# Linear attention and a grouped mixture of experts: the token inputs of each expert take another way into their transposed layout

## The chip, the cores and the metric

One core of one Trainium2 chip. The time is device microseconds of one execution of the whole kernel.

## The reference

```python
def _attn_ref(q, k, v, g_norm):                    # 8 batches, 8 heads, 576 tokens, head size 64
    kv = np.einsum('bhsd,bhse->bhde', k, v)
    out = np.einsum('bhsd,bhde->bhse', q, kv)
    rms = np.sqrt(np.mean(out * out, axis=-1, keepdims=True) + 1e-06)
    return out / rms * g_norm

def _moe_ref(x, w_group, w_expert, w1, w2):        # x: 4608 tokens x 512
    # the group g of a token is the argmax of x @ w_group, its expert e the argmax of x @ w_expert[g];
    # g_w and e_w are the two softmax values of the chosen ones
    for g, e:                                      # 4 x 4 experts
        h = np.maximum(x[tokens] @ w1[g, e], 0.0)  # 512 -> 1024
        out[tokens] = (g_w * e_w)[:, None] * (h @ w2[g, e])   # 1024 -> 512
```

All inputs and the result are float32.

## The kernel before

The first part computes the attention, writes its unnormalised rows with their factors to a DRAM table `scr` (4609 rows of 520 floats), routes the tokens and orders the experts by their number of tokens. The second part, in which the change lies, takes the experts in that order as **regions** 0 to 15. Region r has a fixed capacity CAPS[r] (384, 364, 354, 330, 326, 312, 302, 300, 292, 290, 284, 274, 268, 264, 260, 256 tokens), so all sizes are known when the program is built; what is beyond the capacities goes through a loop at the end. Most of region 0 is done earlier, in plain float32; its last 128 tokens stand at the start of the second part.

Precision: weights and inputs are split into a high part (`whi`, `xh`, `hh`; cast on ScalarE) and a low part (`wlo`, `xl`, `hl`; a subtraction on VectorE), and each product is three matmuls (L305, L306, L310). TensorE does, in each region, layer 1 (8 output chunks f, 4 x 3 matmuls each) into `ps` and layer 2 (4 output chunks d, 8 x 3 matmuls each) into three `psy` buffers.

The order on every engine is the order in the source (a manual schedule); an instruction that waits holds all that stand behind it on its engine. In region r:

- **Inputs of region r + 1.** `gather(r)` fetches token rows from `scr` by three indirect DMAs on GpSimd into `xg` (two buffers). `scale` multiplies them by their factors on GpSimd (L276). `move_x` (L1249), 16 DMAs on SyncE of 32 partitions each, carries quarters of the features to quarters of the partitions, SBUF to SBUF, into `xq` (one buffer), so that `turn_x` (L1254, 32 x 32 block transposes on VectorE) makes the transposed inputs `xt` out of them. `split_x` makes `xh` (L1260) and `xl` (L1261).
- **Results of region r - 1.** `yq` (L1297, one buffer) is the block transpose of `psy` on VectorE; `move_y` (L1268), 16 DMAs on SyncE, brings the quarters back to token rows `yo`, and `scatter_rows` (L252, indirect DMAs on GpSimd) writes them to the result.
- **Weights.** `load_half` (L208) on SyncE loads a half of w1 or w2, 1 MB; `split_piece` (L241 on ScalarE, L242 on VectorE) splits a quarter of a matrix. All raw and split halves rotate through 12 buffers, so a load waits for the split of the half that it replaces.

In layer 2, chunk d is: `split_piece` of the next w1, then (d < 2) two `turn_x`, the matmuls, the `yq` transpose, then `split_x`. SyncE's order in a region is 16 `move_y`, 16 `move_x`, two loads of w2 (f = 3 and 5), two loads of w1 (d = 2 and 3). In region 0 the 16 moves for region 1 are issued in turn by SyncE and ScalarE.

Of the kernel before, what the change touches and what calls it, by code (L numbers as in the profile page):

```python
# [9 lines left out]
F32 = mybir.dt.float32  # L10
# [45 lines left out]
def tile_linattn_moe(ctx: ExitStack, tc: tile.TileContext, qm, qt, k, v, router, w1, w2, out):  # L56
# [27 lines left out]
    RW = DM + H  # L84
    scr = tc.dram_tile([NTOK + 1, RW], F32, name="scr")
    ovt = tc.dram_tile([NBLK, 4], F32, name="ovt")

# [1050 lines left out]
    with ExitStack() as ph:  # L1138
# [81 lines left out]
        def next_psy():  # L1220
            psys.append(psys.pop(0))
            return psys[-1]
# [4 lines left out]
        def moves(cap):  # L1227

            part = [slice(32 * i, 32 * i + 32) for i in range(4)]
            return [(a, s_, part[a], part[s_], len(range(s_, (cap + 31) // 32, 4)))  # L1230
                    for k in range(4) for s_ in range(4) for a in [(s_ + k) % 4]]
# [9 lines left out]
        def scale(r, g):  # L1241
            for j, _ in blocks(CAPS[r]):
                scale_rows(nc.gpsimd, g[0][:, j])

        def move_x(r, g, queues=(nc.sync,)):
            xq = mp.tile([P, 12, P], F32, name="xq", bufs=1)
            pq = xq.rearrange("p (j s) f -> p j s f", s=4)
            for i, (a, s_, pa, ps_, n) in enumerate(moves(CAPS[r])):
                queues[i % len(queues)].dma_start(pq[pa, 0:n, s_, :], g[0][ps_, 0:n, a * P:(a + 1) * P])  # L1249
            return xq, mp.tile([P, KC, 384], F32, name="xt", bufs=1)  # L1250
# [64 lines left out]
        for j, _ in blocks(CAPS[1]):  # L1315
            scale_rows(nc.vector, cur[0][:, j])
        nxt = gather(2)
        ps = next_psy()
        o, h1 = ps[:, 0:DM // 2], st["h"]["h"][:, :, P:2 * P]
# [4 lines left out]
        nc.scalar.activation(out=xT, in_=tp.rearrange("p (c t) -> p c t", c=KC), func=AF.Copy, scale=g2[:, 0:1])  # L1324
        xq, xt = move_x(1, cur, [nc.sync, nc.scalar])
        for i in range(2, 4):
            load_next(i)
        whole2(o, h1, w2c[1], lo=CUT)
# [10 lines left out]

        split_piece(w1n, 0)  # L1340
        for hf in range(2):
            ps = ps_h.tile([P, 512], F32, name="ps")
            whole1(ps, xT, w1c[hf])
            nc.scalar.activation(out=hr[:, hf * 512:(hf + 1) * 512], in_=ps, func=AF.Relu)
            for c in (2 * hf, 2 * hf + 1):
                turn_x(1, xq, xt, c)
                split_x(1, cur, xt, c)
        turn(0)
        turn(1)
        split_piece(w1n, 1)  # L1350
        for x in psys:
# [7 lines left out]
        scatter_rows(yo, P, gidx[:, 0, 2:3])  # L1359
        w1c, w2c = w1n, w2n  # L1360
        nw1, nw2, load_next = weight_loads(eidx[0:1, 2:3])
        for i in range(2):
# [5 lines left out]
        for r in range(1, NE):  # L1368
            cap = CAPS[r]
            _, xh, xl = cur  # L1370
            hh = mp.tile([P, FC, 384], F32R, name="hh", bufs=1)
            hl = mp.tile([P, FC, 384], F32R, name="hl", tag="hl", bufs=1)
            if todo:
                results = move_y(*todo)
            for f in range(FC):
# [7 lines left out]
                if r > 1:  # L1383
                    next(tables, None)
                    next(tables, None)
                if nxt and f == 0:
                    scale(r + 1, nxt)
                    xq, xt = move_x(r + 1, nxt)
                if nxt and f in (3, 5):
                    load_next((f + 1) // 2)  # L1390
                if f >= 3 and results:
                    scatter_rows(*results.pop(0))
                if f == FC - 1 and r + 1 == NE:
                    nc.gpsimd.drain()  # L1394
            nxt2 = gather(r + 2) if r + 2 < NE else None
            nw1a, nw2a, load_a = weight_loads(eidx[0:1, r + 2:r + 3]) if nxt2 else (None, None, None)
# [141 lines left out]
```

## Time and profile before

| | |
|---|---|
| Runs | median 697.4 us (693.17, 697.40, 699.06) |
| Profiled execution | 697.57 us, of which the span of the trace is 695.6 us |
| PE (TensorE matmul) busy | 582.1 us, 84% of the span |
| VectorE (DVE) busy | 368.9 us, 53% |
| ScalarE (ACT) busy | 266.8 us, 38% |
| GpSimd (POOL) busy | 191.4 us, 28% |
| Mean granted TensorE clock | 0.908 |

Busy time is time in which an engine executes; issuing a DMA is not counted. Times in timelines are microseconds from the start of the span. In a timeline line the square brackets tell how long the engine was idle before it and what ended the idleness. SPq and ACTq are the issue of DMAs by SyncE and ScalarE. The granted clock is the TensorE clock as a share of full speed. A DMA share is the mean busy share of the 16 DMA engines.

### The profile page before, as it was taken

How to read it: one execution, taken by the hardware profiler on the slowest of the kernel's cores; microseconds unless marked ns; L12 is line 12 of the kernel's file. 1: busy time of each engine (PE TensorE's matmuls, PEld its weight loads, DVE VectorE, ACT ScalarE, POOL GpSimd, SP SyncE). 2: the span in 40 equal slices, each digit the busy share in tenths (PEclk: the TensorE clock that was granted, in tenths of full speed). 3: DMA queues.
4: the chain of work that ended last, by engine and by line, in shares of the span. 5: the costliest groups of instructions: out<-in, count | busy, mean ns of one | idle time of the engine just before them, and what ended most of it. 6: DMA issues, size and time to landing. Idle time of an engine off the chain costs nothing. (4 is left out here: it accounts for less than half of the span.)

```text
span 695.6 us, 13526 instructions
## 1 busy us (share of the span) xinstructions
PE 582.1 (84%) x5199; PEld 537.0 (77%) x5199; DVE 368.9 (53%) x786; ACT 266.8 (38%) x534; POOL 191.4 (28%) x281
## 2 busy tenths in 40 slices
PE   8889789993799999696979796959696959687795
PEld 4677666871599999696979796959596959687795
DVE  3228868711277764654545545545456464637380
ACT  0356546211253443343434343333334343425260
POOL 4033232340080323223132323131313232221102
PEclk9888999997699999898989898989898989897988
DMA  9999994587036484838484838383838383837331
GB/s 307 379 384 394 335 348 131 198 254 285 0 104 251 117 301 107 301 96 273 116 297 116 310 90 302 96 284 111 291 108 303 91 303 95 300 101 280 89 135 66
DMA packets 74197, 146.95 MB, mean 211 GB/s; under 512 B 12370, under 2 KB 51618, under 8 KB 63122
## 3 DMA queue, kind: packets, MB, share of 16 engines
q1 hardware_dynamic: 65264, 123.51, 51.8%
q0 software_dynamic: 7824, 22.11, 11.2%
q8 instruction: 42, 0.69, 0.4%
q10 hardware_dynamic: 1042, 0.44, 0.3%
q14 instruction: 25, 0.20, 0.1%
HBM read 107.98 MB, written 19.54 MB: 183 GB/s over the span
## 5 line engine op out<-in xcount | busy, mean ns | idle before, releaser
L305 PE MATMUL psy<-hh,whi 128*128 128x364 f32 (+13 forms) x448 | 148.6, 332 | 73.2 <-DVE yq L1297 73.2
L242 DVE TENSOR_TENSOR wlo<-wr,whi 128x1024 fp32r<-128x1024 f32 (+1 forms) x180 | 151.5, 869 | 39.4 <-ACT whi L241 36.0
L305 PEld LDWEIGHTS psy<-hh,whi 128*128 128x128 f32 x448 | 95.1, 212 | 76.1 <-DVE yq L1297 76.0
L306 PE MATMUL psy<-hl,whi 128*128 128x364 f32 (+13 forms) x448 | 146.1, 326 | 0.0
L310 PE MATMUL psy<-hh,wlo 128*128 128x364 f32 (+13 forms) x448 | 145.1, 324 | 0.0
L306 PE MATMUL ps<-xl,whi 128*128 128x364 f32 (+14 forms) x480 | 144.6, 301 | 0.5 <-DVE xl L1261 0.5
L252 POOL DMA_INDIRECT out_dram<-yo,gall x45 | 49.2, 1094 | 346.7 <-DMA xq<-xg 282.7
L305 PE MATMUL ps<-xh,whi 128*128 128x364 f32 (+14 forms) x480 | 144.6, 301 | 0.0
L310 PE MATMUL ps<-xh,wlo 128*128 128x364 f32 (+14 forms) x480 | 144.0, 300 | 0.0
L241 ACT CAST whi<-wr 128x1024 fp32r<-128x1024 f32 (+1 forms) x180 | 128.6, 756 | 0.0
L1260 ACT ACTIVATE xh<-xt,rw 128x364 fp32r<-128x364 f32 (+14 forms) x60 | 32.6, 543 | 199.8 <-DVE xt L1254 199.8
L1254 DVE STREAM_TRANSPOSE xt<-xq 128x320 f32<-128x320 f32 (+4 forms) x60 | 27.1, 487 | 152.4 <-DMA xq<-xg 152.4
L306 PEld LDWEIGHTS psy<-hl,whi 128*128 128x128 f32 x448 | 95.5, 213 | 0.0
L310 PEld LDWEIGHTS psy<-hh,wlo 128*128 128x128 f32 x448 | 94.9, 212 | 0.0
L306 PEld LDWEIGHTS ps<-xl,whi 128*128 128x128 f32 x480 | 90.9, 189 | 0.9 <-DVE xl L1261 0.8
L305 PEld LDWEIGHTS ps<-xh,whi 128*128 128x128 f32 x480 | 90.9, 189 | 0.0
L310 PEld LDWEIGHTS ps<-xh,wlo 128*128 128x128 f32 x480 | 90.7, 189 | 0.0
L279 ACT ACTIVATE hh<-ps 128x364 fp32r<-128x364 f32 (+14 forms) x120 | 50.5, 421 | 101.1 <-PE ps L310 97.8
L280 DVE SCALAR_TENSOR_TENSOR hl<-ps,hh 128x364 fp32r<-128x364 f32 (+14 forms) x120 | 55.2, 464 | 46.8 <-ACT hh L279 46.1
L276 POOL TENSOR_TENSOR xg<-xg 128x256 f32<-128x256 f32 x82 | 52.7, 666 | 26.2 <-DMA xg<-scr,gall 24.5
L248 POOL DMA_INDIRECT xg<-scr,gall x44 | 44.4, 1009 | 13.3 <-issue 13.3
L367 PE MATMUL warm<-wide_b,ones_b 128*128 128x512 bf16 x142 | 42.2, 432 | 2.2 <-POOL wide_b L101 2.2
(255 smaller groups left out, 592.2 us busy)
## 6 DMA issues: line engine op xcount, KB each, us to landing
wr<-in_w_dram SPq DMA_DIRECT2D x64, 1024.0 KB
scr<-xo SPq DMA_DIRECT2D x36, 256.0 KB
m_q<-in_qm_dram SPq DMA_DIRECT2D x8, 1024.0 KB
m_k<-in_k_dram SPq DMA_DIRECT2D x7, 1024.0 KB
m_v<-in_v_dram SPq DMA_DIRECT2D x7, 1024.0 KB
yo<-yq SPq DMA_DIRECT2D x116, 48.0 KB
xq<-xg SPq DMA_DIRECT2D x108, 48.0 KB
xq<-xg SPq DMA_DIRECT2D x124, 32.0 KB
```

The source lines that it names most:

```text
L241: nc.scalar.copy(out=hi, in_=x)
L242: nc.vector.tensor_tensor(out=lo, in0=x, in1=hi.bitcast(F32), op=ALU.subtract)
L248: return nc.gpsimd.indirect_dma_start(out=xg[0:rows, 0:RW], out_offset=None, in_=src, in_offset=bass.IndirectOffsetOnAxis(ap=idx[0:rows, : ...
L252: sc = nc.gpsimd.indirect_dma_start(out=out, out_offset=bass.IndirectOffsetOnAxis(ap=idx[0:rows, :], axis=0), in_=yo[0:rows, :], in_offset ...
L276: eng.tensor_tensor(out=out_[:, hs], in0=x[:, hs], in1=factors(xg)[:, h], op=ALU.mult)
L279: nc.scalar.activation(out=hh, in_=ps, func=AF.Relu)
L280: nc.vector.scalar_tensor_tensor(out=hl, in0=ps, scalar=0.0, in1=hh.bitcast(F32), op0=ALU.max, op1=ALU.subtract)
L305: nc.tensor.matmul(ps, lhsT=stat_h(c), rhs=mov_h(c), start=(c == 0), stop=False)
L306: nc.tensor.matmul(ps, lhsT=stat_h(c), rhs=mov_l(c), start=False, stop=False)
L310: nc.tensor.matmul(ps, lhsT=stat_l(d), rhs=mov_h(d), start=False, stop=(d == n - 1))
L367: nc.tensor.matmul(st["warm"], lhsT=ones_b, rhs=wide_b, start=True, stop=True)
L1260: nc.scalar.activation(out=xh, in_=x, func=AF.Copy, scale=g2[:, 0:1])
```

## The change

A pair of DRAM tables `xd` takes the place of the SBUF-to-SBUF moves of the inputs. `put_x` writes the scaled rows of a region to one of them, 2 KB a row, in up to three DMAs; `get_x` reads `xq` from it in four, one for each quarter of the partitions, in pieces of 512 bytes. In the loop, `get_x(r + 1)` stands at the start of region r ahead of `move_y`; `gather(r + 2)` moves from the end of layer 1 to f = 0, and `scale(r + 2)` and `put_x(r + 2)` stand at f = 1, a region earlier than `scale` and `move_x` did. The scatters of the results begin at f = 5 in place of 3. In region 0, `put_x(1)`, `get_x(1)` and the loads of w2 stand ahead of `gather(2)`, `scale(2)` follows it, `turn_x` and `split_x` for region 1 follow both `turn` calls, `split_piece` of piece 1 moves into the loop over hf, and ScalarE issues none of the transfers. `move_y` stays as it is.

```diff
+    xd = [tc.dram_tile([3 * P, DM], F32, name=f"xd{i}") for i in range(2)]
...
-        def move_x(r, g, queues=(nc.sync,)):
+        def put_x(r, g):
+            for j, rows in blocks(CAPS[r] + -CAPS[r] % 32):
+                nc.sync.dma_start(xd[r % 2][j * P:j * P + rows, :], g[0][0:rows, j, 0:DM])
+
+        def get_x(r):
+            n = (CAPS[r] + 31) // 32
             xq = mp.tile([P, 12, P], F32, name="xq", bufs=1)
-            pq = xq.rearrange("p (j s) f -> p j s f", s=4)
-            for i, (a, s_, pa, ps_, n) in enumerate(moves(CAPS[r])):
-                queues[i % len(queues)].dma_start(pq[pa, 0:n, s_, :], g[0][ps_, 0:n, a * P:(a + 1) * P])
+            for a in range(4):
+                nc.sync.dma_start(xq[32 * a:32 * a + 32, 0:n, :],
+                                  xd[r % 2][0:32 * n, a * P:(a + 1) * P].rearrange("(b i) f -> i b f", i=32))
             return xq, mp.tile([P, KC, 384], F32, name="xt", bufs=1)
...
             scale_rows(nc.vector, cur[0][:, j])
+        put_x(1, cur)
+        xq, xt = get_x(1)
+        for i in range(2, 4):
+            load_next(i)
         nxt = gather(2)
+        scale(2, nxt)
...
-        xq, xt = move_x(1, cur, [nc.sync, nc.scalar])
-        for i in range(2, 4):
-            load_next(i)
...
-        split_piece(w1n, 0)
         for hf in range(2):
+            split_piece(w1n, hf)
             ps = ps_h.tile([P, 512], F32, name="ps")
             whole1(ps, xT, w1c[hf])
             nc.scalar.activation(out=hr[:, hf * 512:(hf + 1) * 512], in_=ps, func=AF.Relu)
-            for c in (2 * hf, 2 * hf + 1):
-                turn_x(1, xq, xt, c)
-                split_x(1, cur, xt, c)
         turn(0)
         turn(1)
-        split_piece(w1n, 1)
+        for c in range(KC):
+            turn_x(1, xq, xt, c)
+            split_x(1, cur, xt, c)
...
         w1c, w2c = w1n, w2n
+        put_x(2, nxt)
         nw1, nw2, load_next = weight_loads(eidx[0:1, 2:3])
...
+            if nxt:
+                xq, xt = get_x(r + 1)
             if todo:
                 results = move_y(*todo)
...
-                if nxt and f == 0:
-                    scale(r + 1, nxt)
-                    xq, xt = move_x(r + 1, nxt)
+                if f == 0:
+                    nxt2 = gather(r + 2) if r + 2 < NE else None
+                if nxt2 and f == 1:
+                    scale(r + 2, nxt2)
+                    put_x(r + 2, nxt2)
                 if nxt and f in (3, 5):
                     load_next((f + 1) // 2)
-                if f >= 3 and results:
+                if f >= 5 and results:
                     scatter_rows(*results.pop(0))
...
-            nxt2 = gather(r + 2) if r + 2 < NE else None
```

## Rows read from the trace of the kernel before

**Rows 1.** The page: busy time of TensorE (time, share of the span, instructions), and the granted TensorE clock in 40 equal slices of the span, in tenths.

```profile
PE 582.1 (84%) x5199; PEld 537.0 (77%) x5199; DVE 368.9 (53%) x786; ACT 266.8 (38%) x534; POOL 191.4 (28%) x281
...
PEclk9888999997699999898989898989898989897988
```

**Rows 2.** The list of waits over the whole span: who waited, for whom, us in total, times, the longest.

```profile
DVE xt L1254 <- DMA xq<-xg: 152.4, 14, 13.4
...
PE psy L305 <- DVE yq L1297: 73.2, 12, 8.2
```

**Rows 3.** The timeline of SyncE's issues in region 8 and into region 9: start, duration, line, transfer, number of issues.

```profile
433.91 10.25 SPq L1268 DMA_DIRECT2D yo<-yq  x16
444.34 11.24 SPq L1249 DMA_DIRECT2D xq<-xg  x16
456.56 8.41 SPq L208 DMA_DIRECT2D wr<-in_w_dram  x4
469.62 0.61 SPq L1268 DMA_DIRECT2D yo<-yq  x1
```

**Rows 4.** The timeline of VectorE in layer 2 of region 8: the first `xt`, the `yq` of the first chunk, the last `wlo` and the last `yq`.

```profile
460.73 0.91 DVE L1254 STREAM_TRANSPOSE xt<-xq 128x320 f32<-128x320 f32 x2 [13.20 <-DMA xq<-xg]
461.56 0.47 DVE L1297 STREAM_TRANSPOSE yq<-psy 128x320 f32<-128x320 f32 x1
...
467.94 1.22 DVE L242 TENSOR_TENSOR wlo<-wr,whi 128x1024 fp32r<-128x1024 f32 x1
469.08 0.51 DVE L1297 STREAM_TRANSPOSE yq<-psy 128x320 f32<-128x320 f32 x1
```

**Rows 5.** Windows: length, busy time (and instructions) of PE, PEld, DVE, ACT and POOL, granted clock, DMA share, GB/s. In this order: regions 1 to 3; after the stall of region 7; region 8; layer 1 of region 4.

```profile
185.40:284.00 98.60, 94.95 (x573) 93.78 (x572) 58.90 (x115) 38.79 (x69) 35.23 (x38) 1.00 0.55 167
...
426.40:431.00 4.60, 4.60 (x18) 4.60 (x19) 4.25 (x8) 3.33 (x6) 0.00 (x0) 0.50 0.95 362
431.93:466.83 34.90, 27.30 (x194) 27.06 (x193) 17.32 (x31) 12.34 (x24) 9.50 (x12) 0.90 0.62 191
...
292.25:306.64 14.39, 14.39 (x97) 14.39 (x97) 10.70 (x26) 6.55 (x14) 0.00 (x0) 1.00 0.43 129
```

**Rows 6.** The timeline of PE: the first matmul after the first, the fifth and the last of the twelve stalls in layer 2.

```profile
286.28 0.64 PE L305 MATMUL psy<-hh,whi 128*128 128x330 f32 x1 [5.42 <-DVE yq L1297]
...
426.38 0.62 PE L305 MATMUL psy<-hh,whi 128*128 128x300 f32 x1 [6.01 <-DVE yq L1297]
...
661.13 0.59 PE L305 MATMUL psy<-hh,whi 128*128 128x260 f32 x1 [5.24 <-DVE yq L1297]
```

**Rows 7.** The issues of two lines on SyncE over the whole span: number, duration in ns (least, median, most), first and last start: a move of 32 partitions (L1249), and a write of 128 rows of 2 KB to DRAM (L560).

```profile
L1249 SPq DMA_DIRECT2D xq<-xg x232: 585/597/1574, 151.3 to 657.8; - x116
...
L560 SPq DMA_DIRECT2D scr<-xo x36: 319/382/1045, 26.5 to 126.0; - x36
```

**Rows 8.** The chain of work that ended last: the landing of the last `move_y` of all, start and duration.

```profile
679.32 2.34 DMA yo<-yq
```

**Rows 9.** DMA queues in two windows: packets, MB, share of 16 engines. First 404 to 411 us, in which nothing but moves is in flight on SyncE's queue; then 418 to 421 us, GpSimd's queue with the gathers.

```profile
q1 hardware_dynamic: 1056, 0.45, 28.7%
...
q0 software_dynamic: 129, 0.36, 51.3%
```

**Rows 10.** Timelines of GpSimd and VectorE: a `scale` beside a busy VectorE at 191.60, one while VectorE waits at 422.64, and the `wlo` at 191.32 beside the first.

```profile
191.60 6.35 POOL L276 TENSOR_TENSOR xg<-xg 128x256 f32<-128x256 f32 x6
...
422.64 3.51 POOL L276 TENSOR_TENSOR xg<-xg 128x256 f32<-128x256 f32 x6 [1.92 <-DMA xg<-scr,gall]
...
191.32 1.35 DVE L242 TENSOR_TENSOR wlo<-wr,whi 128x1024 fp32r<-128x1024 f32 x1 [10.88 <-ACT whi L241]
```

**Rows 11.** Timelines of region 0: ScalarE (its DMA issues, the first `hr`), PE (the end of layer 1, the three stalls), VectorE (the last scaling of the rows, the first `xt`, the last `xl`, the copies of `hT`, the fills of `psy`).

```profile
158.12 6.96 ACTq L1249 DMA_DIRECT2D xq<-xg  x8
...
166.39 0.60 ACT L1344 ACTIVATE hr<-ps 128x512 f32<-128x512 f32 x1
...
159.69 1.02 PE L294 MATMUL ps<-wr,xT 128*128 128x512 f32 x2
167.04 1.11 PE L1337 MATMUL ps<-ident,hr 128*128 128x128 f32 x4 [6.33 <-ACT whi L241]
174.04 1.11 PE L1337 MATMUL ps<-ident,hr 128*128 128x128 f32 x4 [5.88 <-ACT hr L1344]
180.21 9.72 PE L298 MATMUL psy<-wr,hT 128*128 128x256 f32 x32 [5.05 <-DVE psy L1352]
...
149.82 0.76 DVE L276 TENSOR_TENSOR xg<-xg 128x256 f32<-128x256 f32 x2 [2.79 <-DMA xg<-scr,gall]
...
170.54 0.58 DVE L1254 STREAM_TRANSPOSE xt<-xq 128x384 f32<-128x384 f32 x1 [2.80 <-DMA xq<-xg]
...
177.04 0.60 DVE L1261 SCALAR_TENSOR_TENSOR xl<-xt,rw,xh 128x364 fp32r<-128x364 f32 x1 [0.67 <-ACT xh L1260]
177.56 1.28 DVE L1338 COPY hT<-ps 128x512 f32<-128x512 f32 x2
...
179.99 0.45 DVE L1352 MEMSET psy<- 128x128 f32 x3
```

## The prediction

> **What bounds the kernel now.** I read four views in order.
>
> First the page: PE counts 84% busy, with a granted clock that swings between 0.8 and 0.9 in the second half [rows 1]. So PE nearly sets the time, but something stops it again and again.
>
> Then the list of waits: PE sits 73.2 us, in 12 waits, in front of the first layer-2 product of a `psy` buffer, released by the `yq` transpose on VectorE; VectorE itself sits 152.4 us, in 14 waits, in front of `turn_x` for the moved inputs `xq` [rows 2]. The reader should put the two together: `yq` stands behind `turn_x` in VectorE's order, so PE runs out of its three `psy` buffers when `xq` is late.
>
> Then the timelines of one region, r = 8, engine by engine. SyncE issues 16 `move_y` transfers from 433.91 (10.4 us), 16 `move_x` transfers from 444.34 (11.2 us), then the four weight loads [rows 3]. VectorE starts `xt` at 460.73 and ends its `yq` of block 3 at 469.6; SyncE starts the next `move_y` at 469.62 [rows 3, 4]. So the region is a ring: 10.4 (issue y) + 11.2 (issue x) + 5.2 (455.6 to 460.7, landing) + 8.9 (VectorE's work of layer 2) = 35.7 us, which is 433.91 to 469.62. PE's own work is shorter: 96 products of 326 columns take 14.39 us at full clock [rows 5], 0.46 ns a column, so a region of capacity C needs 192 x C x 0.46 ns: 28.8 us at 326, 25.8 at 292, 24.2 at 274, 23.0 at 260.
>
> Last, what a stall costs beyond its length. The 12 stalls run from region 3 (ends 286.28) to region 14 (ends 661.13); the one of region 7 ends at 426.38 [rows 6]. After it the granted clock is 0.50 until 431.0 [rows 5]: 18 products in 4.6 us that take half of it at full clock, so 2.3 us more.
>
> **The change part by part.** The execution profiled took 697.6 us, its span and 2.0 us around it; the median of the runs is 697.4, so no shift is needed.
>
> *The 16 `move_x` leave the ring.* `put_x` runs two regions ahead of use and `get_x` at the start of the region before use, so `xq` is due at the middle of a region (11.5 to 14 us after its start) and its four reads are issued in the first 3 us. `turn_x` no longer waits. Gain: 73.2 us of PE idle, plus 12 x 2.3 = 27.6 us of half clock; 100.8 us, if nothing else becomes late.
>
> *What is late next.* `move_y` still has 16 issues, now behind `get_x`, and `yq` (one buffer) can't be rewritten before `move_y` has read it. That is a new, shorter ring: last `wlo` of layer 2, weight load issued (0.4), four `get_x`, `move_y` 10.4 [rows 3], landing, then VectorE from `yq` of block 0 (461.56) to the last `wlo` (469.2), 7.6 us [rows 4]. No read of this shape is in the trace. A move of 32 partitions issues in 0.597 us, and a write of 128 rows, 256 KB, in 0.38 [rows 7], so size doesn't drive the issue: I take 0.6 for each `get_x` (2.4 us), and 1.8 as far end, should it go with the number of 512-byte pieces, three times a move's. Landing is 2.3 us with the queue empty [rows 8] and 5.2 in the ring above. Ring: 0.4 + 2.4 + 10.4 + 2.3 + 7.6 = 23.1 us, which only region 14 (23.0) feels. With the landing of 5.2 it is 26.0 us, above PE's need in regions 8 to 14 by 0.2, 0.4, 0.9, 1.8, 2.3, 2.7 and 3.0: 11 us. I take the middle, **6 us given back**.
>
> *DMA traffic.* Region 8 keeps the engines 0.62 x 34.9 = 21.6 us busy [rows 5]. `get_x` reads as many 512-byte pieces as the moves did, about 1,280; a window of moves alone shows 1,056 packets for 28.7% of 7 us on 16 engines, 30 ns each [rows 9], so it is 2.4 us for 2.4 us. `put_x` adds 0.66 MB; at the rate of the gathers beside it (0.36 MB for 51.3% of 3 us [rows 9]) 2.8 us. So 24.4 us a region, above PE's need only in regions 11 to 14, by 3.4 us in all: inside the 6.
>
> *Waits added.* `put_x(r+2)` waits on SyncE for `scale` on GpSimd; behind it are queued the loads of w2. GpSimd gathers and scales for r + 2 as soon as its scatters are out, by my estimate 15 to 28 us into the region before (`move_y` landed at 13 to 15, then three scatters and three gathers, their landing and a scale), so SyncE, which reaches `put_x` about 13 us into its region, finds it done by several microseconds; w2 loads leave then at 15 us and are wanted 23 us or more into the region. If that cover is gone, each us of lateness beyond it is a us per region. `get_x(r+1)` waits for a write made a region earlier: nothing. The scatters at f = 5 to 7 wait for `move_y` (landed 15 us in) as before; in the last region it was so at f = 3 too.
>
> *`scale` now runs beside a busy VectorE.* Where that happened before (191.60) six took 6.35 us, against 3.51 in a stall of VectorE; the `wlo` beside it took 1.35 us against 1.22 [rows 4, 10]. Four such are 0.5 us a region: within the 6. The Trainium skill, "SBUF — State Buffer", section "Who interferes with whom", speaks against the change here: a VectorE operation with two SBUF inputs and a GpSimd operation that reads SBUF exclude each other on a shared port, so VectorE might lose all of the 3.5 us; by that the ring would be 26.6 us and 16 us would be given back in place of 6 (a time of 604). The row bears out that both get slower, but VectorE by a tenth; I keep the row.
>
> *The start (region 0).* Now ScalarE spends 158.12 to 165.1 on 8 issues of moves, and `hr` of the first half, whose product PE had long done, comes only at 166.39; `turn_x` waits for `xq` till 170.54; PE, done at 160.7, sits 6.33, 5.88 and 5.05 us and starts layer 2 of region 0 at 180.21 [rows 11]. After: the scaled rows are there at 150.6; three writes (0.4 each) and a landing of 2.3 to 5.2 us, four reads (2.4) and again a landing give `xq` at about 159 to 164. PE goes from the second half (160.7) straight to `turn`, 0.6 + 1.1 + 0.6 us with `hr` and the copy, 163. Then the four `xt`/`xl` steps, 170.54 to 177.6 [rows 11], 7.0 us, and the fills, 0.45: PE goes on at 170.6. One stall of 8 us in place of 17.3; 9.6 us earlier, of which I take 9 (4 if `xq` lands 5 us later, 13 if the product after it keeps full clock).
>
> *The end.* Region 15 has no moves of x; its chain (`move_y`, scatters, drain) is as before. Nothing.
>
> Sum: 697.6 - 100.8 - 9 + 6 = 593.8, **594 us**.
>
> **Rivals.**
>
> *The `move_y` ring takes over for good.* If `get_x` issues at 1.8 us, the ring is 27.9 us with a short landing: given back, over regions 5 to 14, 28 us; with the long one 30.8 us, 58 us over regions 4 to 14 and some 9 x 2.3 of half clock, 78. So 616 to 667, say **640**. For it: SyncE's issues are what the old ring is made of. Against: rows 7.
>
> *The queue fills (the other side).* All of SyncE's transfers go through one queue. If a 512-byte read from DRAM cost what a packet of the gathers does, 0.513 x 3 x 16 / 129 = 191 ns [rows 9], `get_x` would hold the engines 1,280 x 191 / 16 = 15.3 us a region in place of 2.4, and the region would need 37.3 us, against 34.1 on average now ((661.13 - 286.28) / 11 [rows 6]): 12 x 3.2 - 9, **727 us**. It is slower than before from about 160 ns. Against: those packets are up to eight times as large, and shared the engines with the moves.
>
> *The clock gives way.* PE would work 390 us nearly without a gap. If the granted clock fell to 0.9, that is 43 us: **637**. Against: regions 1 to 3, from 185.4 to 284, hold 1.00 with PE busy 95 of 98.6 us [rows 5]. The Trainium skill, "TensorE: Matmul & The Clock Gate", section "What's actually happening", says that idleness lowers the clock and activity restores it, and this trace agrees (0.50 after each stall); no run here yet shows 390 us on end.
>
> *It doesn't do what it says.* The wait put down to `xq` may be another's (a weight load, VectorE's own work), and the moves only hide it: **about 690**. Against: VectorE idles 13.2 us right before `xt`, its own earlier work done [rows 4].
>
> **How the numbers follow.** The forecast, with its terms' bounds (582 with 13 at the start and nothing given back, 612 with 4 and 20): 0.76. `move_y` ring 0.11, clock 0.04, queue 0.04, no effect 0.05. The range reaches into the `move_y` ring: **582 to 625**. One per cent is about what a measurement of this kernel tells from no change; faster by more than that 0.92, within it 0.03, slower 0.05.
>
> **What would show it.** Right: no wait of VectorE for `xq` from region 2 on, twelve PE waits gone or under 3 us, granted clock near 1.0 from 190 on, regions of 23 to 29 us, PE's pause in region 0 about 8 us, no transfers issued by ScalarE after the start. In the last regions, small waits of VectorE at `yq` for the transfer `yo<-yq`. Wrong: `get_x` issues near 2 us; SyncE standing at `put_x` for `scale`; DMA at 0.95 or more throughout; PE waiting for weights (`ps` before `whi`), which would say that the weight loads, not the inputs, come last.

## The result, and the profile after

The changed kernel takes **624.56 us** (median of four runs, 623.63 to 625.29) where the kernel before takes 695.28 (four runs, 691.22 to 699.06): a ratio of 0.898, with an interval of 0.892 to 0.904. The profiled execution took 625.3 us, its span 623.6. It is faster, and inside the range given, but only 0.4 us under its upper end: 30.8 us above the forecast of 593.8 by the median, 31.5 in the profiled execution, on which the sums below are made.

The page of the changed kernel, busy time of each engine and the 40 slices of granted clock and of DMA share; the first two lines answer to [rows 1].

```profile
PE 562.0 (90%) x5181; PEld 521.1 (84%) x5199; DVE 375.3 (60%) x786; ACT 267.2 (43%) x534; POOL 210.3 (34%) x281
...
PEclk9898999999889999999999999979998979798999
DMA  8999995648867769596959595969687777859541
```

TensorE is at 90% in place of 84. From slice 13 on the clock is full but for dips behind the new stalls, in slices 27 to 37. From slice 16 to 29 the DMA row alternates, 9 and then 5 or 6: the engines are full, and then half empty.

The waits of the changed kernel over the whole span (who, for whom, us in total, times, the longest); the second line answers to the PE row of [rows 2].

```profile
DVE yq L1303 <- DMA yo<-yq: 62.9, 10, 7.6
...
PE psy L306 <- DVE yq L1303: 22.4, 8, 4.2
...
PE psy L299 <- DVE psy L1359: 10.3, 1, 10.3
```

PE's 73.2 us in 12 waits are 22.4 in 8. The wait of VectorE for `xq`, 152.4 us, is gone from the head of the list. In its place VectorE stands 62.9 us at `yq` until `move_y` of the region before has read the buffer.

Where the time went by region: the table is worked out from PE's timeline, as the differences between the first layer-1 products of successive regions; "need" is the forecast's 192 x C x 0.46 ns, all in us. The last two columns are experiments told below.

| region | C | need | before | after | e11 | e7 |
|---|---|---|---|---|---|---|
| 1 | 364 | 32.2 | 32.6 | 32.6 | 32.2 | 32.2 |
| 2 | 354 | 31.3 | 32.0 | 32.0 | 32.0 | 32.0 |
| 3 | 330 | 29.1 | 38.1 | 28.6 | 28.6 | 28.6 |
| 4 | 326 | 28.8 | 37.2 | 28.8 | 28.8 | 28.8 |
| 5 | 312 | 27.6 | 34.1 | 27.4 | 27.4 | 27.4 |
| 6 | 302 | 26.7 | 33.7 | 26.5 | 26.5 | 26.5 |
| 7 | 300 | 26.5 | 34.7 | 29.0 | 26.8 | 26.3 |
| 8 | 292 | 25.8 | 34.9 | 33.3 | 26.4 | 26.2 |
| 9 | 290 | 25.6 | 34.4 | 28.2 | 27.0 | 26.1 |
| 10 | 284 | 25.1 | 33.4 | 30.2 | 25.6 | 25.6 |
| 11 | 274 | 24.2 | 34.4 | 30.8 | 24.3 | 24.3 |
| 12 | 268 | 23.7 | 33.8 | 29.6 | 25.4 | 23.9 |
| 13 | 264 | 23.3 | 32.6 | 29.1 | 25.0 | 23.1 |
| 14 | 260 | 23.0 | 31.2 | 26.7 | 24.3 | 23.0 |
| 1 to 14 | | 372.7 | 476.9 | 412.6 | 380.2 | 373.9 |

Up to region 6 the changed kernel runs at PE's own pace. From region 7 on, where PE's need is 26.5 us and less, it doesn't follow: a region stays at 27 to 33 us, as if something else took some 30. The forecast for the fourteen was 476.9 - 100.8 + 6 = 382.1, so 30.5 of the 31.5 us are here; the rest is mainly region 0.

Now the stage itself. SyncE's issues in the changed kernel from region 10 into region 11 (start, duration, line, transfer, number), which answer to [rows 3]:

```profile
454.60 16.92 SPq L1274 DMA_DIRECT2D yo<-yq  x16
471.64 1.48 SPq L1248 DMA_DIRECT2D xd<-xg  x3
473.39 2.78 SPq L209 DMA_DIRECT2D wr<-in_w_dram  x4
476.35 2.54 SPq L1254 DMA_DIRECT2D xq<-xd  x4
480.69 21.44 SPq L1274 DMA_DIRECT2D yo<-yq  x16
502.24 1.48 SPq L1248 DMA_DIRECT2D xd<-xg  x3
```

The sixteen `move_y`, 10.25 us before, take 16.92 and 21.44. And the four weight loads, 1 MB each, spread over 8.41 us before, leave together, in 2.78 us, right ahead of the next `get_x` and `move_y`. VectorE of the changed kernel at both ends of the same ring (the brackets are the idle time before, and what ended it), which answer to [rows 4]:

```profile
473.21 0.48 DVE L1303 STREAM_TRANSPOSE yq<-psy 128x288 f32<-128x288 f32 x1 [7.26 <-DMA yo<-yq]
...
503.61 0.48 DVE L1303 STREAM_TRANSPOSE yq<-psy 128x288 f32<-128x288 f32 x1 [7.13 <-DMA yo<-yq]
```

From one to the other is 30.4 us: 7.5 of VectorE's work until `move_y` starts (473.21 to 480.69), 21.4 of `move_y` issues, and 1.5 until `yq` may be written. That is the ring which the forecast named, at 23.1 to 26.0. The chain of waits of the changed kernel between the two says what stretched the issues:

```profile
476.35 18.14 DMA xq<-xd
494.50 0.58 SPq L1274
...
501.53 1.86 DMA yo<-yq
```

A `get_x` issued at 476.35 lands 18.14 us later, and a `move_y` goes out the moment it has; the eleven issues after it follow at 0.6 us each. The last move lands in 1.86 us. So SyncE doesn't work on `move_y` for 21 us; it is held, in two ways, which are told apart below.

Windows of the changed kernel: length, busy time of PE, PEld, DVE, ACT and POOL, granted clock, DMA share, GB/s. In this order: regions 1 to 3 and the first third of 4, which answer to [rows 5]; the 22 us after the bunched loads; the stretch behind the stall that follows; regions 7 to 14.

```profile
185.00:284.00 99.00, 99.00 (x620) 99.00 (x619) 72.46 (x147) 46.19 (x82) 39.84 (x42) 1.00 0.77 237
...
473.00:495.00 22.00, 21.25 (x155) 21.25 (x155) 17.19 (x30) 11.10 (x21) 10.79 (x11) 0.92 0.94 308
...
502.20:511.00 8.80, 6.85 (x38) 6.85 (x39) 7.37 (x13) 3.42 (x6) 5.46 (x5) 0.63 0.89 304
357.90:594.60 236.70, 212.67 (x1538) 209.97 (x1537) 144.67 (x258) 103.90 (x193) 82.57 (x84) 0.94 0.77 247
```

While `get_x` is under way the DMA engines are 94% busy, with four loads (4.2 MB), the moves and GpSimd's gathers and scatters. After the stall the granted clock is 0.63 over 8.8 us, and over regions 7 to 14 it is 0.94: 6% of 236.7 us, or some 14 us by this estimate, lost beside the 22.4 of idle time.

### The profile page after: what moved, and what is told of

Its sections match the earlier page's. It is cut to its first block, busy times and chain, and to the rows that moved or that the text cites. A ratio compares the mean times of both kernels' runs of the same rounds, so it can differ in the third digit from the quotient of the medians.

```text
span 623.6 us, 13421 instructions
## 1 busy us (share of the span) xinstructions
PE 562.0 (90%) x5181; PEld 521.1 (84%) x5199; DVE 375.3 (60%) x786; ACT 267.2 (43%) x534; POOL 210.3 (34%) x281
## 4 chain that ended last, share of the span: by engine, by line
DMA 37%; PE 36%; SPq 14%; DVE 7%; issue 5%; ACT 1%; POOL 0%; POOLq 0%; DVEq 0%
DMA xq<-xd 20%; SPq L1274 12%; DMA wr<-in_w_dram 7%; PE warm L368 4%; DMA yo<-yq 3%; PE ps L311 3%; PE ps L307 3%; PE ps L306 3%; PE psy L311 3%; PE psy L307 3%; PE ops L521 3%; PE psy L306 3%; PE l L295 2%; DVE wlo L243 2%; PE kps L474 2%
## 5 line engine op out<-in xcount | busy, mean ns | idle before, releaser
L243 DVE TENSOR_TENSOR wlo<-wr,whi 128x1024 fp32r<-128x1024 f32 (+1 forms) x180 | 156.2, 895 | 36.6 <-ACT whi L242 34.4
L306 PE MATMUL psy<-hh,whi 128*128 128x364 f32 (+13 forms) x448 | 141.3, 315 | 22.4 <-DVE yq L1303 22.4
L307 PE MATMUL psy<-hl,whi 128*128 128x364 f32 (+13 forms) x448 | 140.3, 313 | 0.0
L311 PE MATMUL psy<-hh,wlo 128*128 128x364 f32 (+13 forms) x448 | 140.2, 313 | 0.0
L306 PEld LDWEIGHTS psy<-hh,whi 128*128 128x128 f32 x448 | 89.8, 201 | 24.2 <-DVE yq L1303 24.2
L277 POOL TENSOR_TENSOR xg<-xg 128x256 f32<-128x256 f32 x82 | 59.9, 755 | 93.2 <-DMA xg<-scr,gall 93.1
L307 PEld LDWEIGHTS psy<-hl,whi 128*128 128x128 f32 x448 | 89.9, 201 | 0.0
L311 PEld LDWEIGHTS psy<-hh,wlo 128*128 128x128 f32 x448 | 89.8, 200 | 0.0
L1266 ACT ACTIVATE xh<-xt,rw 128x364 fp32r<-128x364 f32 (+14 forms) x60 | 32.6, 543 | 118.3 <-DVE xt L1260 105.3
L1303 DVE STREAM_TRANSPOSE yq<-psy 128x320 f32<-128x320 f32 (+3 forms) x56 | 28.4, 508 | 80.1 <-DMA yo<-yq 62.9
L249 POOL DMA_INDIRECT xg<-scr,gall x44 | 57.3, 1302 | 13.3 <-issue 13.1
L368 PE MATMUL warm<-wide_b,ones_b 128*128 128x512 bf16 x124 | 37.0, 428 | 4.1 <-POOL wide_b L102 2.2
```

Of the source, the lines that this page charges most:

```text
L243: nc.vector.tensor_tensor(out=lo, in0=x, in1=hi.bitcast(F32), op=ALU.subtract)
L249: return nc.gpsimd.indirect_dma_start(out=xg[0:rows, 0:RW], out_offset=None, in_=src, in_offset=bass.IndirectOffsetOnAxis(ap=idx[0:rows, : ...
L277: eng.tensor_tensor(out=out_[:, hs], in0=x[:, hs], in1=factors(xg)[:, h], op=ALU.mult)
L306: nc.tensor.matmul(ps, lhsT=stat_h(c), rhs=mov_h(c), start=(c == 0), stop=False)
L307: nc.tensor.matmul(ps, lhsT=stat_h(c), rhs=mov_l(c), start=False, stop=False)
L311: nc.tensor.matmul(ps, lhsT=stat_l(d), rhs=mov_h(d), start=False, stop=(d == n - 1))
```

## The experiments

One more thing has to be known of the program, as it is built: every transfer issued by SyncE or ScalarE counts on one of eight semaphores, taken in turn, and an issue waits until the transfer eight before it, on the same semaphore, has landed. (Above, the fifth `move_y` goes out at 494.50; the first `get_x`, eight issues before it, lands at 494.49.) GpSimd's transfers have eight of their own. In the changed kernel the order around a region's start is, with what each is made to wait for:

```
order on SyncE     waits for the landing of
get_x 1..4         put_x 1..3 and the move ahead of them
move_y 1..4        the four weight loads
move_y 5..8        get_x 1..4
move_y 9..16       move_y 1..8
```

SyncE's waits for these landings in the changed kernel, ahead of `move_y` (L1274), over the whole span:

```profile
SPq L1274 <- DMA wr<-in_w_dram: 26.7, 15, 4.1
...
SPq L1274 <- DMA xq<-xd: 10.3, 9, 3.1
```

These waits are idle time of SyncE ahead of an issue. They are the smaller part of the hold: summed from the timeline over regions 7 to 14, they come to 28 us at `move_y`. Another 39 us there are in issues that last up to 7.85 us in place of 0.6, and `get_x` has 23 us of the same kind; mostly these are the last `get_x` or the first `move_y` behind the loads. In the ring shown above, the first `move_y` takes 7.85 of the 21.44 us. The issues of the two lines in this stretch (number, duration in ns: least, median, most):

```profile
L1274 SPq DMA_DIRECT2D yo<-yq x128: 585/596/7850, 360.6 to 587.5; - x128
...
L1254 SPq DMA_DIRECT2D xq<-xd x32: 160/564/7350, 356.5 to 567.7; - x32
```

What holds an issue while it lasts, the trace doesn't tell.

The experiments went through three theories. The first (Q) was SyncE's one queue, in which `move_y` stands behind the weight loads, so that another issuer for the loads would cure it; its rival (B) was engines full of bytes, which no order of the transfers cures. When e1, e2 and e4 had missed the times of Q (e2 and e4 came out about where B had them), the turn of the eight semaphores was put to the test (S): the loads hold the moves by their semaphores. B fell only with e7. The last (C) is the collision: the loads leave in a bunch just ahead of the small transfers, which land late among them and then hold the issues.

All ratios below are to the kernel before on the same chip, whose medians were 691 to 694 us. "After" is the changed kernel; every edit but those of e8 and e10 is made to it.

**e1: the weight loads leave SyncE.** ScalarE issues those of regions 3 on.

```diff
-            nw1a, nw2a, load_a = weight_loads(eidx[0:1, r + 2:r + 3]) if nxt2 else (None, None, None)
+            nw1a, nw2a, load_a = weight_loads(eidx[0:1, r + 2:r + 3], nc.scalar) if nxt2 else (None, None, None)
...
-                if nxt and f in (3, 5):
-                    load_next((f + 1) // 2)
+                if nxt and f in (5, 7):
+                    load_next((f - 1) // 2)
```

> The changed kernel, with the weight loads of regions 3 to 15 issued by ScalarE in place of SyncE (the two of w2 at f = 5 and 7, after the splits that they wait for). Theory Q (queue): the 4 MB of weights stand in SyncE's queue ahead of get_x and move_y, and move_y gets through only when they have drained; without them the move_y ring is about 21 us, shorter than PE's need everywhere, PE's waits before psy in regions 7 to 14 vanish, 590 to 595 us. Theory I (issue, the ring of the prediction): only four issues of 0.34 us leave the ring, 1.4 us a region in eight regions, about 612 us. Theory B (the DMA engines are full): the same bytes on the same engines, 624 us.

Measured: 645.36 us (638.39 to 647.16), 0.935 (0.931 to 0.940). Slower than the changed kernel, which was not expected. The waits of e1, over the whole span:

```profile
ACT whi L242 <- DMA yo<-yq: 68.6, 11, 9.4
...
PE psy L306 <- ACT hh L280: 28.1, 10, 6.0
```

ScalarE, which now issues loads, is held until moves of results have landed (the eight semaphores are shared with SyncE), its own work `hh` comes late, and PE waits for that. `move_y` still takes long: 16.06 us from 460.10, in region 10. So the idea of one crowded queue, which another issuer relieves, fell.

**e2: `move_y` ahead of `get_x`.**

```diff
-            if nxt:
-                xq, xt = get_x(r + 1)
             if todo:
                 results = move_y(*todo)
+            if nxt:
+                xq, xt = get_x(r + 1)
```

> The changed kernel, with get_x behind move_y in SyncE's order. Q: move_y still stands behind the weights but no longer behind the reads of xq (2 us of issue, and 2 to 3 us in the queue): 2 to 5 us a region in eight regions, 590 to 608 us. I: the ring loses the 2 us of issue, about 608 us. B: 624 us.

Measured: 621.6 us (620.03 to 624.53), 0.899 (0.894 to 0.903): as the changed kernel. The wait has only changed its place: VectorE of e2 waits for `xq`.

```profile
DVE xt L1260 <- DMA xq<-xd: 72.3, 13, 8.8
...
PE psy L306 <- DVE yq L1303: 15.5, 8, 3.1
```

Whichever of the two groups stands behind the loads pays for them.

**e3: the early place without the DRAM.** From region 2 on the sixteen SBUF moves of the kernel before stand at `get_x`'s place, and there is no `put_x`.

```diff
+        def move_x(r, g, queues=(nc.sync,)):
+            xq = mp.tile([P, 12, P], F32, name="xq", bufs=1)
+            pq = xq.rearrange("p (j s) f -> p j s f", s=4)
+            for i, (a, s_, pa, ps_, n) in enumerate(moves(CAPS[r])):
+                queues[i % len(queues)].dma_start(pq[pa, 0:n, s_, :], g[0][ps_, 0:n, a * P:(a + 1) * P])
+            return xq, mp.tile([P, KC, 384], F32, name="xt", bufs=1)
...
-                xq, xt = get_x(r + 1)
+                xq, xt = move_x(r + 1, nxt)
...
-                    put_x(r + 2, nxt2)
```

> The changed kernel, but from region 2 on the inputs go by the 16 old moves, SBUF to SBUF, where get_x stands (ahead of move_y, a region early), without put_x. It asks whether the early place or the 3 + 4 transfers bring the gain. I: 12 issues of 0.64 us more in the ring, 31 us a region, about 675 us. Q: the same and the weights ahead of them, 680 to 720 us. If only the early place mattered: 620 to 630 us.

Measured: 680.62 us (677.39 to 686.34), 0.986 (0.978 to 0.995). The early place, with the new start still in, is worth some 10 us (4 to 15) of the 70; the rest comes with the way through DRAM and its few transfers. SyncE of e3 from the end of region 8 shows which group is held now: `move_x`, first behind the loads, takes 19.02 us, and `move_y` behind it 10.20, its plain issue time.

```profile
441.91 0.92 SPq L209 DMA_DIRECT2D wr<-in_w_dram  x2
443.07 19.02 SPq L1250 DMA_DIRECT2D xq<-xg  x16
462.26 10.20 SPq L1281 DMA_DIRECT2D yo<-yq  x16
```

**e4: one load fewer ahead.** The second half of w1 is loaded after the next region's `move_y`.

```diff
                 results = move_y(*todo)
+            if nxt and r > 1:
+                load_next(1)
...
-                    if n >= 2 and nxt2:
-                        load_a(n - 2)
+                    if n == 2 and nxt2:
+                        load_a(0)
```

> The changed kernel, with the second half of w1 loaded after move_y of the next region in place of at the end of layer 2, on SyncE as before: three of the four loads stand ahead of move_y in the queue. Q: 2.7 us a region less in eight regions, about 603 us, unless the half then comes late for its split. I and B: no change, 620 to 626 us.

Measured: 629.81 us (624.89 to 632.86), 0.910 (0.903 to 0.918). No gain. VectorE of e4 waits less at `yq`, but ScalarE now waits for the weights:

```profile
ACT whi L242 <- DMA wr<-in_w_dram: 69.6, 32, 5.1
...
DVE yq L1303 <- DMA yo<-yq: 36.6, 9, 5.5
```

A load put later than its collision is wanted before it can arrive.

**e6: the weight loads issued by GpSimd**, whose transfers count on semaphores of their own, so that `move_y` waits for no weight load. The w2 loads go out at f = 5 and 7, as in e1.

```diff
-            nw1a, nw2a, load_a = weight_loads(eidx[0:1, r + 2:r + 3]) if nxt2 else (None, None, None)
+            nw1a, nw2a, load_a = weight_loads(eidx[0:1, r + 2:r + 3], nc.gpsimd) if nxt2 else (None, None, None)
```

> As e1, but the weight loads of regions 3 to 15 are issued by GpSimd, whose transfers count on semaphores of their own. Theory S (rotation), formed after e1: the transfers of SyncE and ScalarE count on eight semaphores in turn, and each issue waits until the transfer eight issues before it has landed; in the changed kernel the eight before the first eight move_y are the four weight loads and the four get_x, so move_y waits for 4 MB of weights; on ScalarE the loads kept their places in the rotation, so there they waited for move_y. S: with GpSimd the move_y issues wait for moves alone, 590 to 605 us. Q (one queue, drained in order) gave the same for e1 and missed it. B (full engines): 624 us. GpSimd could become late instead, since a load that waits for its split holds the gathers behind it: then 610 to 640 us with waits of SyncE at put_x.

Measured: 638.67 us (637.67 to 646.99), 0.926 (0.918 to 0.934). The time lies where a late GpSimd was expected, but the sign named for it is missing: SyncE stands at `put_x` no longer than in the changed kernel. The waits for weights went, and waits for `get_x` took their place on SyncE. The first of SyncE's waits in e6, over the whole span:

```profile
SPq L1274 <- DMA xq<-xd: 88.3, 31, 5.8
```

`move_y` takes 19.06 us from 458.93. So it isn't the semaphores' turn with the weights alone. The long issues are nearly gone (in regions 7 to 14 none of `get_x` lasts over 0.6 us, none of `move_y` over 1.21), but the waits ahead of `move_y` come to 69 us there: one kind of hold has taken the place of the other.

**e9: e6, and `get_x` issued by GpSimd too.** SyncE's eight semaphores then carry only `move_y`, `put_x` and the first regions' loads.

```diff
-                xq, xt = get_x(r + 1)
+                xq, xt = get_x(r + 1, nc.gpsimd)
```

> As e6, with the four get_x too issued by GpSimd: in the rotation of eight stand only move_y and put_x, so no move_y waits for the landing of weights or of get_x. S: the 16 issues of move_y take 10 to 11 us again in the regions from 7 on (21 in the changed kernel, 16 to 19 in e1 and e6), and yq no longer waits; the time is 590 to 605 us if GpSimd keeps up. If the issues still take 16 us or more, the rotation is not what holds them (the engines or the queue are), 625 to 640 us. GpSimd now issues 14 to 17 transfers a region; if it is late, that shows as waits of VectorE for xq or of ScalarE for weights instead, with move_y short.

Measured: 619.73 us (613.57 to 625.5), 0.892 (0.883 to 0.901), which can't be told from the changed kernel. SyncE of e9: its waits, all span.

```profile
SPq L1274 <- DMA yo<-yq: 97.0, 76, 5.7
```

A `move_y` waits 76 times for a `move_y` eight before it, and the sixteen still take 17.72 us from 449.49. With nothing else in their turn they hold each other, which they can only do if each lands late. Beside them run the weight loads: over 420.6 to 440.3, one of these stretches, the DMA engines of e9 are at 0.92. A small transfer beside bulk ones lands several us late, whoever issued the bulk. The ring hardly stops PE any more in e9: its wait behind `yq` is down to 4.0 us in all. But ScalarE now waits 43.4 us for the weights that GpSimd issues:

```profile
ACT whi L242 <- DMA wr<-in_w_dram: 43.4, 20, 4.4
...
PE psy L306 <- DVE yq L1303: 4.0, 4, 1.4
```

**e7: results through DRAM as well.** `move_y` becomes four writes (`put_y`) and, two steps of layer 1 later, two reads (`get_y`); `put_x` is two writes in place of three. SyncE issues 16 transfers a region in place of 27, with more bytes (165.9 MB in all against 156.7).

```diff
-        def move_y(r, yq):
+        def put_y(r, yq):
+            n = (CAPS[r] + 31) // 32
+            for a in range(4):
+                nc.sync.dma_start(yd[r % 2][0:32 * n, a * P:(a + 1) * P].rearrange("(b i) f -> i b f", i=32),
+                                  yq[32 * a:32 * a + 32, 0:n, :])
+            return r
+
+        def get_y(r):
...
+            nc.sync.dma_start(yo[:, 0:2], yd[r % 2][0:2 * P, :].rearrange("(j p) f -> p j f", p=P))
+            if rest:
+                nc.sync.dma_start(yo[0:rest, 2], yd[r % 2][2 * P:2 * P + rest, :])
...
-                results = move_y(*todo)
+            ry = put_y(*todo) if todo else None
...
+                if ry and f == 2:
+                    results = get_y(ry)
```

> The changed kernel, with the results too moved through a pair of DRAM tables: 4 writes by quarters and 2 reads in place of the 16 move_y, and put_x in 2 writes in place of 3; SyncE issues 16 transfers a region in place of 27. S and I: SyncE is through in about 9 us, the loads leave when their splits allow it and have landed when the rotation comes round to them, 590 to 605 us, PE waits before psy gone. B: 0.66 MB more a region on full engines, 635 to 645 us.

Measured: **588.6 us** (585.76 to 590.03), 0.851 (0.846 to 0.855), just under the 590 to 605 expected and the best of all versions. Two windows of e7 (columns as above), region 11, and from the start of region 1 to the end of the last region's products:

```profile
461.80:486.20 24.40, 24.40 (x195) 24.40 (x194) 19.09 (x32) 12.96 (x24) 13.66 (x12) 1.00 0.95 325
...
182.30:578.00 395.70, 395.70 (x2882) 395.57 (x2880) 284.52 (x506) 195.61 (x358) 160.12 (x158) 1.00 0.88 280
```

PE works 395.7 of 395.7 us at full clock. It does so with more bytes, and in region 11 with the DMA engines 95% busy: so the changed kernel isn't slow because its engines are full of bytes. SyncE of e7 in the same stretch as shown above:

```profile
462.54 4.96 SPq L1276 DMA_DIRECT2D yd<-yq  x4
...
472.97 7.96 SPq L210 DMA_DIRECT2D wr<-in_w_dram  x4
481.04 2.35 SPq L1257 DMA_DIRECT2D xq<-xd  x4
```

The four loads are spread over 7.96 us again, held by VectorE as each buffer comes free, because SyncE reaches them in time.

**e10: results through DRAM, inputs by the sixteen moves of the kernel before.** An edit to the kernel before, with `put_y` and `get_y` as in e7:

```diff
-                results = move_y(*todo)
+            ry = put_y(*todo) if todo else None
...
+                if ry and f == 2:
+                    results = get_y(ry)
```

> The kernel before, with the results alone moved through DRAM (4 writes, 2 reads) and the 16 moves of the inputs where they were. The old ring of 35.7 us loses 12 issues of 0.64 us, 7.7 us: 28 us a region, unless the rotation makes the first move_x wait for the weights in turn. By the ring alone: stalls of 1 to 5 us in regions 5 to 14, 615 to 635 us. With the weights ahead of move_x as they stood ahead of move_y: 640 to 665 us. If it isn't the number of transfers of SyncE that counts: 690 us.

Measured: 666.99 us (660.41 to 669.27), 0.961 (0.955 to 0.967). VectorE of e10 waits for `xq` again (first two lines, all engines), and SyncE for the gathers (the waits of SyncE):

```profile
DVE xt L1255 <- DMA xq<-xg: 109.5, 12, 12.6
...
PE psy L306 <- DVE yq L1306: 50.6, 10, 7.8
```

```profile
SPq L1250 <- DMA xg<-scr,gall: 79.9, 15, 8.9
```

The time is next to what the expectation had for moves held by weights, but not for that reason: `move_x` takes 10.27 us from 451.30, unheld. It starts late, since SyncE stands for the rows of the next region, which are gathered in the same one. Taking out the sixteen transfers of the results brings 27 us, taking out those of the inputs, putting the rest a region earlier and changing the start 70, both 103 (692 to 589).

**e8: the new start alone,** in the kernel before: `put_x(1)` and `get_x(1)` at the start, ScalarE without issues, the new order of `turn_x` and `split_piece`, the moves of the other regions as they were.

```diff
+        put_x(1, cur)
+        xq, xt = get_x(1)
+        for i in range(2, 4):
+            load_next(i)
...
-        xq, xt = move_x(1, cur, [nc.sync, nc.scalar])
-        for i in range(2, 4):
-            load_next(i)
```

> The kernel before, with the changed start alone (region 0: inputs of region 1 through DRAM, nothing issued by ScalarE, the new order of turn_x and split_piece); the loop from region 1 on is that of before. The trace of the changed kernel puts the start 7.5 us earlier (region 1 begins at 182.05 against 189.58): 7 to 8 us faster than before, ratio 0.989.

Measured: 691.63 us (ten runs, 682.27 to 694.5), 0.9947 (0.9903 to 0.9991). That is 3.7 us of gain, between 1 and 7. It is less than the 7 to 8 that were expected from the start of region 1, 7.5 us earlier in the changed kernel's trace than in that of the kernel before. But that difference of two traces holds more than the change: e10, with the old start, begins region 1 at 181.53, and e8, with the new one, at 188.30. Counted from the end of PE's layer 1 of region 0, region 1 begins 28.9 us later in the kernel before and 22.9 in e10, with the same program up to there; in the ten traces with the new start it is 18.4 to 21.3. So the new start is worth 2 to 10 us by these traces, and 3.7 fits. Why the old start differs by 6 us between two traces stays open.

**e11: the same transfers, the bunch broken up.** The 27 transfers of the changed kernel, its bytes and its one issuer stay. The two loads of w2 go out between the moves, after the eighth and after the twelfth `move_y`; `put_x` moves behind the second of them.

```diff
-            for a, s_, pa, ps_, n in moves(CAPS[r]):
+            for k, (a, s_, pa, ps_, n) in enumerate(moves(CAPS[r])):
+                if k in (8, 12):
+                    yield
                 nc.sync.dma_start(yo[ps_, 0:n, a * P:(a + 1) * P], pq[pa, 0:n, s_, :])
...
-                    put_x(r + 2, nxt2)
                 if nxt and f in (3, 5):
                     load_next((f + 1) // 2)
+                if part and f in (3, 5):
+                    results = next(part)
+                if nxt2 and f == 5:
+                    put_x(r + 2, nxt2)
```

> The changed kernel with the same 27 transfers of SyncE a region, the same bytes and the same queue, but the two loads of w2 leave between the issues of move_y (after the eighth and after the twelfth) and put_x stands behind move_y at f = 5. Theory C (collision), formed after e9: SyncE reaches its four loads only after move_y and put_x, so 4 MB leave in 3 us and the next region's get_x and move_y land behind them; with eight semaphores in turn no more than eight transfers are in flight, so a late landing holds the issue, whichever queue the weights are in. C: with w2 gone out 5 to 10 us earlier only 2 MB stand ahead of the next move_y, its 16 issues take 11 to 15 us in place of 16 to 21 in regions 7 to 14, and the time is 595 to 612 us. B (the engines are simply full): 620 to 626 us, the same.

Measured: 600.86 us (595.0 to 603.35), 0.868 (0.861 to 0.875), as the collision theory said and outside what full engines would give. SyncE of e11, from the end of region 10, the same stretch of work as shown of the changed kernel:

```profile
461.76 2.29 SPq L1254 DMA_DIRECT2D xq<-xd  x4
466.46 6.25 SPq L1276 DMA_DIRECT2D yo<-yq  x8
473.46 0.36 SPq L209 DMA_DIRECT2D wr<-in_w_dram  x1
473.87 3.45 SPq L1276 DMA_DIRECT2D yo<-yq  x4
477.58 0.37 SPq L209 DMA_DIRECT2D wr<-in_w_dram  x1
478.00 2.51 SPq L1276 DMA_DIRECT2D yo<-yq  x4
480.62 1.47 SPq L1248 DMA_DIRECT2D xd<-xg  x3
483.19 0.95 SPq L209 DMA_DIRECT2D wr<-in_w_dram  x2
486.72 2.40 SPq L1254 DMA_DIRECT2D xq<-xd  x4
```

From the first `move_y` to the end of the last it is 14.05 us with two loads among them, where the changed kernel needs 21.44 for the moves alone. The ring by e11's chain of waits, from `yq` to `yq` (the chain ends the last wait by `put_x`, which is issued right behind the last `move_y`):

```profile
458.98 0.48 DVE yq L1305
...
480.62 3.33 DMA xd<-xg
483.95 0.47 DVE yq L1305
```

That is 25.0 us (7.5 + 14.05 + 3.4) in place of 30.4 in the same two regions, against PE's need of 24 to 25. No wait of PE for `yq` of more than half a us is left, so regions 7 to 14 take 204.8 us in all against 236.7. What e11 doesn't tell apart is how much of this comes from the earlier loads and how much from the later `put_x`.

## Why the forecast was right, and where it was off

**The ring of the kernel before: right.** `turn_x` hardly waits for `xq` any more (4.7 us in place of 152.4), regions 3 to 6 lost their stalls whole, and PE runs at 192 x C x 0.46 ns there, within 0.6 us a region. e3 shows that the early place isn't enough for it: with sixteen transfers at that place 680.6 us remain.

**What is late next: the right ring, the wrong size.** This is the step that failed. The forecast named the ring through `move_y` and `yq`, gave it 23.1 to 26.0 us, and 6 us given back. It measured 30.4 us from region 10 to region 11, and in regions 1 to 14 together 36.5 us were given back (412.6 against 476.9 - 100.8): 22.4 us of PE's idle time in eight stalls, and the 14 us of lower clock behind them. Term by term: VectorE's 7.6 is 7.5; the load and `get_x`, 2.8, lie beside VectorE's work here and cost this ring nothing (in five of the eight regions from 7 on a long last `get_x` put `move_y` off by 1.0 to 5.4 us); the landing at the end, 2.3, is 1.9. The term that was mis-sized is **`move_y`, taken at 10.4 us of issue and measured at 15.6 to 21.4** in regions 7 to 14. In the trace of the kernel before it took 10.2 to 12.0 us in every region, but what the sixteen issues take depends on what is in flight beside them.

**Why it stretched: "w2 loads leave then at 15 us".** That sentence costed an edit at nothing and named its cover, and the cover wasn't there. In region 10 (starts at 448.34) they left at 473.4, 25 us in, because `move_y` and `put_x` ahead of them on SyncE ended only then. By that time the buffers of the next w1 were free as well, so four loads went in 2.8 us and the next `get_x` and `move_y` landed among them: 18.1 us for a `get_x` for which the forecast had at most 5.2. Behind the loads the issues were held in both ways, by waits for the eight semaphores and by issues that last up to 7.85 us, and late `move_y` makes the next loads late in turn. That the bunch is the cause is shown by e11 (same transfers, loads apart and `put_x` later: 601 us), and e7 fits it (fewer transfers, loads spread by themselves: 589). The rivals are out: another issuer for the loads is no cure (e1 645, e6 639), nor the order of the small groups (e2 622); nor are the engines too full for the bytes of a region (e7 moves more of them). The Trainium skill, "DMA: Bandwidth & Descriptors", section "Issuing engines are not separate DMA queues", says that transfers from all issuers run on the same 16 engines and interleave, and that more issuers save sequencer time alone; e1, e6 and e9 agree, with 16.1, 19.1 and 17.7 us for `move_y` beside loads that SyncE no longer issued. Where the issuer changed, the long issues of `get_x` went and the semaphores' waits grew (e6), so neither kind of hold is the cause by itself. Whether more than eight semaphores would help isn't settled: no run here had more.

**The start: 9 us forecast, 7.5 between the two traces.** Region 1 begins at 182.05 instead of 189.58, a difference that holds more than the change (e8). PE's one pause is 10.3 us, not 8, since `xq` was there at 165.5, not at 159 to 164: the chain gives the landing of `put_x` 7.06 us and that of `get_x` 5.51, where 2.3 to 5.2 was taken for each. That is the same mistake in small, a landing taken from a stage with other transfers in flight. By itself the new start shows 3.7 us (e8).

**`scale` and `put_x`: right.** In the changed kernel the six operations of a `scale` take 4.51 us (at 491.48), between the two of [rows 10], and the `wlo` beside them 1.50 in place of 1.22: VectorE is slowed, not stopped for the length of a `scale`. SyncE stands at `put_x` for `scale` only once, in region 1, 5.1 us for its three writes.

**The rivals.** The queue doesn't fill with 512-byte reads: e7 reads and writes DRAM in such pieces for inputs and results and meets PE's need in each of the fourteen regions within 0.8 us. The clock doesn't give way: 395.7 us of unbroken work at 1.00 (e7). The Trainium skill, "TensorE: Matmul & The Clock Gate", section "What's actually happening", says that activity releases the throttle, and e7 agrees. "It doesn't do what it says" fell with VectorE's wait for `xq`. The `move_y` ring taking over, forecast at 640, is nearest to what happened; but its condition, `get_x` issues of 1.8 us each for their pieces, wasn't met (median 0.54 us; the four for region 3 take 1.99). Behind the loads the four took up to 10.5 us, nearly all of it in the last one. It came by another way.

**Luck.** The forecast's own terms reach from 582 to 612 us (584 to 613, as its terms add up), and 624.56 lies outside them. It lies in the stretch up to 625 that was added for the `move_y` rival, whose mechanism wasn't the one that came. That the range still holds the time is luck.

## What to carry to other kernels

When a ring of many small transfers is removed, look for the next ring and price its issues not by their duration in the old trace, but by what will be in flight beside them: bulk loads that the new order makes leave together held the small transfers behind them here. Place each bulk load where its buffer comes free, between the small transfers if need be (625 to 601 us with the same transfers), before trying another issuer (639 and 645). Here fewer transfers beat fewer bytes: a detour through DRAM with more bytes and 16 transfers a region in place of 27 reached 589.

## What the hardware showed that was not expected

A 144 KB read took 18.1 us to land behind 4 MB of loads, though the engines then moved 308 GB/s; by that rate 4.2 MB take 13.6 us. One issue of SyncE behind such loads lasted 7.85 us, where the median is 0.6. In e9 moves of 32 or 48 KB held one another by up to 5.7 us beside loads that another engine had issued, where the last one of the changed kernel's chain, with the loads through, landed in 1.9.
